# A planned kernel on one core: a transfer queue in the plan, filler products as plan steps, and a newly searched order

## Chip, core and metric

The kernel runs on one core of a Trainium2 chip. The metric is the device time of one execution in microseconds (us); the median over the runs of a comparison is quoted. A single-core program's run is called slow here when it is more than 1.5% above the fastest run of the same kernel in the same comparison, otherwise fast. Ratios between kernels are computed from the mean time of the fast runs of one kernel over the mean of the fast runs of the other, from the same rounds on the same chip. They are therefore not quite the ratio of the medians that are quoted beside them.

## The reference

A recurrent attention over 4 batches, 8 heads, 768 positions and 48 channels feeds a token mixer:

```
for t in range(S):
    cur   = outer(u * k[t], v[t])
    y[t]  = r[t] @ (state + cur)
    state = w[t] * state + outer(k[t], v[t])
x     = y, heads side by side                        # 4 x 768 x 384
W     = (x @ w_q) @ (x @ w_k)^T / sqrt(64)
out   = relu(W @ x) @ w_out
```

The inputs r, k, v and w are float32; the output is 4 x 768 x 384 float32.

## The kernel before

The positions are cut into twelve units of 256 (three for each batch; numbered 0 to 11 here). Per unit there are four loads of 384 KB (w, k, r, v into wg, kg, rg, vg, three buffers each). ScalarE takes the logarithm of w (step f_ln, tile lw), TensorE sums it over positions (f_cw), and from that come the decays en and ep, the scaled and transposed KT and RT, the products A of KT and RT, their masked form AM, the state SB, the output y and the mixer input X. After the third unit of a batch come the mixer's products T, mx and fp, and the stores.

The order of all instructions on all engines is fixed on the host by a list scheduler. A step has an engine, an estimated duration, a rank and the steps that it needs; buffers are rings.

```python
class Plan:
    def add(self, eng, dur, rank, fn, after=(), fill=None, read=(), lag=100, mode=0, behind=None):
        ...
    def order(self):
        ...                       # of the ready steps of a free engine, the lowest rank starts
```

Each engine executes its steps strictly in the planned order. The plan decides once which step comes before which.

```python
def load(b, i, tl, ap):
    nc.sync.dma_start(out=view(tl, 0, [[D2, H], [1, D2]]),
        in_=ap[b, :, ds(i * U, U)].rearrange("h (p j) d -> p h (j d)", j=2))
...
add("SP", 1250 + (900 if n == 0 else 0), "load", lambda: load(b, i, wg, w),
    fill="wg", got=g["wg"], lag=2000)
# ... kg, rg and vg likewise
def f_ln():
    nc.scalar.activation(view(lw, ...), view(wg, ...), ACT.Ln, bias=0.0, scale=math.exp(-MU))
add("A", 845, "ln", f_ln, fill="lw", got=g["lw"], use=[g["wg"]])
...
nc.vector.memset(Z, 0.0)
for _ in range(WARM):                             # nine fillers at the head, on the zero tile
    mm(PS[:, ds(0, 512)], Z[:, ds(0, C)], Z)
...
for s in plan.order():
    now["step"] = s
    s["fn"]()
```

Of the kernel before, what the change touches and what calls it, by code (L numbers as in the profile page):

```python
# [12 lines left out]
F32 = mybir.dt.float32  # L13
# [12 lines left out]
class Plan:  # L26
# [11 lines left out]
    def add(self, eng, dur, rank, fn, after=(), fill=None, read=(), lag=100, mode=0,  # L38
# [6 lines left out]
            self.reads(s, a)  # L45
        return s

    def reads(self, s, a, own=False):

        if not own:  # L50
            s["after"].append(a)
        if a["buf"] is not None:
            a["buf"]["left"] += 1
            s["reads"].append(a["buf"])

    def order(self):
# [22 lines left out]

        ready = [s for s in self.steps if not left[s["n"]]]  # L80
        running, done, eng_free, now = [], [], {}, 0
        mode = 0
        while ready or running:
            ready.sort(key=lambda s: (s["rank"] - self.stick * (s["eng"] == "PE"
                                                                and s["mode"] == mode), s["n"]))
# [1 line left out]
            while started:  # L87
                started = False
                for s in ready:
                    if s["behind"] is not None and "start" not in s["behind"]:  # L90
                        continue
                    if ready_at[s["n"]] > now or eng_free.get(s["eng"], 0) > now:
                        continue
                    if s["fill"] in ("w", "s"):
                        at = place(s["fill"])
                        if at is None:
                            continue
                        s["buf"]["bank"] = at
                        for x in range(at[0], at[0] + at[1]):
                            banks[x] = False  # L100
                    elif s["fill"] is not None:

                        ring, size = rings.setdefault(s["fill"], []), self.kinds[s["fill"]]
                        if len(ring) >= size and ring[-size]["left"]:
                            continue
                        ring.append(s["buf"])
                    took = s["dur"]
                    if s["eng"] == "PE":
                        took += self.switch * (s["mode"] != mode)
                        mode = s["mode"]  # L110
                    eng_free[s["eng"]] = now + took
                    heapq.heappush(running, (now + took + s["lag"], s["n"]))
                    s["start"] = now
                    done.append(s)
                    ready.remove(s)
                    started = True
                    break
# [6 lines left out]
            while running and running[0][0] <= now:  # L124
                t, n = heapq.heappop(running)
                s = self.steps[n]
                for buf in s["reads"]:
                    buf["left"] -= 1
                    if not buf["left"]:
                        for x in range(buf["bank"][0], sum(buf["bank"])) if "bank" in buf else ():  # L130
                            banks[x] = True
                for o in s["out"]:
                    left[o["n"]] -= 1
                    ready_at[o["n"]] = max(ready_at[o["n"]], t)
                    if not left[o["n"]]:
                        ready.append(o)
# [5 lines left out]
def kernel(  # L142
# [41 lines left out]
        return consts.tile(shape, dtype, name=name, tag=name)  # L184

    PS = ps.tile([C, 4096], F32, name="PS", tag="PS")
    WARM = 9
    NB = 3
    WG = [const([C, HW], F32, f"wg{i}") for i in range(NB)]
    RG = [const([C, HW], F32, f"rg{i}") for i in range(NB)]  # L190
# [35 lines left out]
    gv = const([C, 1], F32, "gv")  # L226

    nc.vector.memset(Z, 0.0)
    for _ in range(WARM):
        mm(PS[:, ds(0, 512)], Z[:, ds(0, C)], Z)  # L230
    nc.vector.memset(uT, 0.0)
    for hh in range(2):
        nc.scalar.dma_start(out=view(uT, hh, [[2, NP], [1, 1]], p0=hh * 64, pn=D),
# [37 lines left out]
    for j in range(2):  # L271
# [5 lines left out]

    NS = 2
    STEP = 100
    OFF = dict(load=-149, ln=901, c16=248, cw=-84, ex=-742, rT=1166, ks=886, qT=-1499, RT=731,  # L280
               KT=349, ptm=181, v16=-272, vp=114, vb=422, dps=395, vd=320, A=-667, am=556,
               kb=545, kd=-134, sn=-139, sb=91, y=278, x=-1392, xt=770, xts=808, qk=1219,
               qks=-111, T=-1307, mx=141, rl=-837, fp=-3204, os=-81, st=20, stick=99)
    ENG = dict(k16="PPPPPPPPPPDP", r16="PPPPPPPAPPDD", KT="DPPPPPPPPPPP", vb="AAAADAAAAAAA",
               kd="ADAAADADDADA", xts="DADAADAADAAA", qks="AAAAADAAAAAD", rl="DAAAAAAAADAD",
               os="AAAAAAAAAADD", dd="ADAADDDDAAAA", ks="DDADDDDDADAD")
    SPLIT = (0, B * NU - 1)
    NAMES = dict(A="ACT", D="DVE", P="POOL")

# [18 lines left out]
    def took(eng, cols, half=False, by=False):  # L308
        if eng == "A":
            return (265 if by else 180) + int(cols * 0.83)  # L310
        if eng == "P":
            return 100 + int(cols * 1.93)
        return (210 if by else 150) + int(cols * (0.52 if half else 1.04))

    def copy(eng, o, i, by=None):
# [13 lines left out]
        else:  # L329
            nc.vector.tensor_scalar_max(o, i, 0.0)  # L330

    def warm(at, count, after):

        def f():
            x = stile(F32, "warm")
            for _ in range(count):
                mm(x, ID16, Z)
        s_ = plan.add("PE", 215 * count, at, f, after, fill="s", lag=100)
        plan.reads(s_, s_, True)

    class Got:

# [10 lines left out]
    def unit(n, state, batch):  # L353
# [41 lines left out]
        def cols(cs, w_):  # L395
# [1 line left out]

        g = {x: Got() for x in ("wg kg rg vg lw k16 r16 v16 vp cw ep en kT rT ks qT RT KT ptm VB dps dd Vd"
                                " A0 A1 AM0 AM1 kb KD sn y xt XT qk").split()}
        add("SP", 1250 + (900 if n == 0 else 0), "load", lambda: load(b, i, wg, w), fill="wg", got=g["wg"], lag=2000)  # L400
        add("SP", 1250, "load", lambda: load(b, i, kg, k), fill="kg", got=g["kg"], lag=2000)
        add("SP", 1250, "load", lambda: load(b, i, rg, r), fill="rg", got=g["rg"], lag=2000)

        add("SP", 1250, "load", lambda: load(b, i, vg, v), fill="vg", got=g["vg"], lag=2000)

        def f_ln():
            nc.scalar.activation(view(lw, 0, [[64, H], [512, 2], [1, D]]),  # L407
# [4 lines left out]
        def f_c16(dst, src, e):  # L412
# [3 lines left out]
                   view(src, 0, [[D2, H], [D, 2], [1, D]]))  # L416
            return f
        e = ENG["k16"][n]
        add(e, 500 if e == "D" else 830, "c16", f_c16(k16, kg, e), fill="k16", got=g["k16"],
            use=[g["kg"]])  # L420
        e = ENG["r16"][n]
        add(e, 500 if e == "D" else 830, "c16", f_c16(r16, rg, e), more=1, fill="r16", got=g["r16"],
            use=[g["rg"]])

        def f_cw():
# [108 lines left out]
        for cs in fine:  # L534
            def f_vd(cs=cs):
                nc.gpsimd.tensor_tensor(  # L536
                    sb("Vd", [C, 2 * DM])[:, cols(cs, DM)], t["VB"][:, cols(cs, DM)],
                    view(t["dd"], cs[0] * H, [[1, len(cs) * H], [0, D]]), ALU.mult)
            add("P", took("P", DM * len(cs)), "vd", f_vd, more=2 * cs[0], fill="Vd", got=g["Vd"],
                cs=cs, use=[g["VB"], g["dd"]])  # L540

        for c in range(2):
# [178 lines left out]
        for ii in range(NU):  # L721
            m = b * NU + ii
            gm, gM, gf, go = Got(), Got(), Got(), Got()
            if end and ii == 0:
                warm(STEP * n + OFF["mx"] - 1, 2, Tall)

            def f_mx(ii=ii):
                t[f"mx{ii}"] = x = wtile("mx")
# [3 lines left out]
                       start=(dt != 1))  # L732
            add("PE", 330, "mx", f_mx, Ts + batch["wq"], more=6 * ii, fill="w", got=gm)

            if end and ii == NU - 1:
                warm(STEP * n + OFF["mx"] + 6 * ii + 1, 2, [gm.first])
            halves = each if end else both
            for p, cs in enumerate(halves):
                e = "AD"[p] if end else ENG["rl"][m]
# [23 lines left out]
            for p, cs in enumerate(halves):  # L763
# [15 lines left out]
                if end and ii == NU - 1 and p == 0:  # L779
                    add("A", 550, "st", f_st(nc.scalar), more=6 * ii, cs=cs, use=[go], lag=2000)  # L780
                else:
                    add("SP", 650 * len(cs), "st", f_st(nc.sync), more=6 * ii, cs=cs, use=[go],
                        lag=2000)

    state = {}
    batch = None
# [18 lines left out]
    for n in range(B * NU):  # L805
        if n % NU == 0:
            batch = {"X": {}, "qks": [], "wq": [], "xs": []}
        if n == 0:
            wl = plan.add("SP", 2500, 105, f_wld, lag=2000)
            state["ub"] = plan.add("POOL", 200, 12, f_ub)  # L810
            state["wts"] = plan.add("POOL", 1800, 120, f_wcast, [wl])
        unit(n, state, batch)
# [33 lines left out]
```

## Time and profile before

| | before |
|---|---|
| median of 3 runs (range) | 120.91 us (118.89 to 121.9) |
| profiled run; its span and mean TensorE clock | 119.73 us; 118.0 us, 0.952 |
| TensorE busy in the span | 101.0 us (86%) |
| TensorE idle from 20 to 108 us | 9.0 us |
| last load issued | 70.70 us |

The page and windows are shown and read in the prediction. The waits: who waited for whom; total us, times, longest.

```profile
ACT lw L407 <- DMA wg<-in_w_dram: 8.7, 6, 2.4
```

Then the queue of SyncE in time (start, us until its issue ended, what it moved): two stores, a third store, and the w loads of units 10 and 11.

```profile
44.37 1.60 SPq L774 DMA_DIRECT2D out_dram<-os  x2
...
49.93 0.38 SPq L774 DMA_DIRECT2D out_dram<-os  x1
...
61.17 1.20 SPq L213 DMA_DIRECT2D wg<-in_w_dram  x1
...
66.38 1.89 SPq L213 DMA_DIRECT2D wg<-in_w_dram  x1
```

And ScalarE's own timeline of lw for those two units, with some of its neighbours; the bracket is idle time of the engine just before, and what ended it.

```profile
63.27 1.02 ACT L438 ACTIVATE en<-PS 128x1024 bf16<-128x1024 f32 x1
64.19 1.04 ACT L444 ACTIVATE ep<-PS 128x1024 bf16<-128x1024 f32 x1
66.35 0.84 ACT L407 ACTIVATE lw<-wg 128x768 bf16<-128x768 f32 x1 [1.12 <-DMA wg<-in_w_dram]
67.10 0.78 ACT L318 CAST VB<-PS 128x768 bf16<-128x768 f32 x1
...
71.90 0.84 ACT L407 ACTIVATE lw<-wg 128x768 bf16<-128x768 f32 x1
```

So before also waits for loads on ScalarE, 8.7 us in six pieces, but near the end of the loads only 1.12 us, and the last not at all.

### The profile page before, as it was taken

To read this page: it belongs to the slowest core of one execution; us is meant where nothing else is said; L and a number is where in the kernel's file an instruction comes from. 1 tells how busy PE (TensorE), PEld (TensorE's weight loads), DVE (VectorE), ACT (ScalarE), POOL (GpSimd) and SP (SyncE) were. 2 spreads that over 40 slices of the span, in tenths; PEclk is the share of its full clock that TensorE was granted. 3 is DMA by queue.
4 is the path that set the end of the run, shared out by engine and by line. 5 is a ranking of instruction groups with operands and counts; after the bars stand their busy time and mean duration, and the time that the engine had idled before them with its cause. 6 is when DMAs were issued, how large, how long until landed. Compare 5 with 4: busy or idle time off the path is not lost. (4 is left out here: it accounts for less than half of the span.)

```text
span 118.0 us, 3685 instructions
## 1 busy us (share of the span) xinstructions
PE 101.0 (86%) x1496; PEld 69.8 (59%) x1496; DVE 89.9 (76%) x143; ACT 80.9 (69%) x120; POOL 75.5 (64%) x95
## 2 busy tenths in 40 slices
PE   5858988796987999793999389999999999998980
PEld 2344957473865666482878246667678776673440
DVE  6837897977798768979499696978789996761460
ACT  4375497786955698676899664758999638675630
POOL 6485789999996998883916999370794580050000
PEclk9985599999999999999999976999999999999998
DMA  2999999999999999999998999533120000523064
GB/s 55 306 316 314 320 292 250 313 288 280 315 293 285 310 244 237 363 341 249 244 280 225 319 273 272 138 133 133 43 96 0 6 0 0 190 85 133 0 230 172
DMA packets 54865, 24.61 MB, mean 209 GB/s; under 512 B 51392, under 2 KB 54848, under 8 KB 54848
## 3 DMA queue, kind: packets, MB, share of 16 engines
q1 hardware_dynamic: 54288, 24.19, 72.5%
q10 hardware_dynamic: 560, 0.20, 0.7%
q8 instruction: 11, 0.18, 0.6%
q14 instruction: 6, 0.05, 0.1%
HBM read 19.66 MB, written 4.72 MB: 207 GB/s over the span
## 5 line engine op out<-in xcount | busy, mean ns | idle before, releaser
L554 DVE TENSOR_TENSOR AM<-PS,US 128x1024 bf16<-128x1024 f32 x24 | 28.8, 1218 | 4.0 <-PE PS L173 3.1
L487 POOL TENSOR_TENSOR KT<-ks,en 128x1024 bf16<-128x1024 bf16 (+1 forms) x12 | 23.8, 1988 | 2.3 <-ACT en L438 1.1
L536 POOL TENSOR_TENSOR Vd<-VB,dd 128x768 bf16<-128x768 bf16 (+1 forms) x14 | 18.0, 1292 | 9.3 <-ACT dd L318 8.8
L407 ACT ACTIVATE lw<-wg 128x768 bf16<-128x768 f32 x12 | 10.2, 846 | 8.8 <-DMA wg<-in_w_dram 8.7
L438 ACT ACTIVATE en<-PS 128x1024 bf16<-128x1024 f32 (+1 forms) x14 | 12.6, 904 | 4.8 <-PE PS L173 3.4
L641 DVE SCALAR_TENSOR_TENSOR X<-PS,gx,Vd 128x768 bf16<-128x768 f32 (+1 forms) x13 | 12.4, 953 | 4.4 <-PE PS L173 2.2
L173 PEld LDWEIGHTS <-KT 48*128 48x128 bf16 (+1 forms) x272 | 11.0, 100 | 5.7 <-POOL KT L487 1.8
L501 POOL CAST v<-vg 128x768 bf16<-128x768 f32 x12 | 10.2, 854 | 5.9 <-PE PS L173 5.6
L415 POOL CAST k<-kg 128x768 bf16<-128x768 f32 x11 | 9.1, 824 | 7.4 <-PE PS L173 4.3
L173 PE MATMUL PS<-wo,MX 128*128 128x384 bf16 x72 | 13.3, 327 | 0.0
L600 DVE TENSOR_TENSOR SB<-PS,ptm 128x384 bf16<-128x384 f32 x20 | 11.0, 552 | 2.6 <-PE PS L173 1.8
L444 ACT ACTIVATE ep<-PS 128x1024 bf16<-128x1024 f32 (+1 forms) x14 | 12.9, 922 | 0.0
L318 ACT COPY os<-PS 128x768 f32<-128x768 f32 (+1 forms) x12 | 8.5, 722 | 4.4 <-PE PS L173 4.4
L328 ACT ACTIVATE MX<-PS 128x768 bf16<-128x768 f32 (+1 forms) x11 | 8.0, 724 | 4.5 <-PE PS L173 4.5
L173 PE MATMUL PS<-qk,ts 128*128 128x256 bf16 x36 | 10.2, 406 | 0.1
L173 PE MATMUL PS<-RT,KT 48*128 48x128 bf16 x192 | 8.8, 227 | 1.5 <-POOL KT L487 1.5
L173 PE MATMUL PS<-CM,lw 64*128 64x128 bf16 x192 | 7.6, 221 | 2.8 <-DVE X L641 1.8
L173 PE MATMUL PS<-VB,AM 128*128 128x48 bf16 x192 | 8.5, 185 | 1.6 <-DVE AM L554 1.0
L318 ACT CAST VB<-PS 128x768 bf16<-128x768 f32 x11 | 8.8, 802 | 1.4 <-POOL wq L797 0.7
L173 PEld LDWEIGHTS <-AM 128*128 128x128 bf16 x192 | 7.5, 97 | 3.2 <-issue 1.1
L173 PEld LDWEIGHTS <-MX 128*128 128x128 bf16 x72 | 6.5, 98 | 4.7 <-issue 0.3
L173 PEld LDWEIGHTS <-lw 64*128 64x128 bf16 x192 | 5.7, 96 | 5.5 <-issue 3.1
(81 smaller groups left out, 213.3 us busy)
## 6 DMA issues: line engine op xcount, KB each, us to landing
wg<-in_w_dram SPq DMA_DIRECT2D x12, 384.0 KB, 5.1
kg<-in_k_dram SPq DMA_DIRECT2D x12, 384.0 KB, 5.3
rg<-in_r_dram SPq DMA_DIRECT2D x12, 384.0 KB, 5.6
vg<-in_v_dram SPq DMA_DIRECT2D x12, 384.0 KB, 5.4
out_dram<-os SPq DMA_DIRECT2D x9, 384.0 KB, 3.7
out_dram<-os SPq DMA_DIRECT2D x5, 192.0 KB, 2.0
wof<-in_moe_w_out_dram SPq DMA_DIRECT2D x1, 576.0 KB, 4.5
out_dram<-os ACTq DMA_DIRECT2D x1, 192.0 KB, 2.2
```

The lines of the kernel that those rows point to most:

```text
L173: nc.tensor.matmul(o, l, rr, start=start, stop=stop, skip_group_check=True, is_transpose=trans)
L318: nc.scalar.copy(o, i)
L407: nc.scalar.activation(view(lw, 0, [[64, H], [512, 2], [1, D]]), view(wg, 0, [[D2, H], [D, 2], [1, D]]), ACT.Ln, bias=0.0, scale=math.exp( ...
L415: op(view(dst, 0, [[64, H], [512, 2], [1, D]]), view(src, 0, [[D2, H], [D, 2], [1, D]]))
L438: nc.scalar.activation(sb("en", [C, 1024])[:, cols(cs, 512)], t["cw"][:, cols(cs, 512)], ACT.Exp, bias=0.0, scale=-1.0)
L444: nc.scalar.activation(view(ep, cs[0] * NP * EW + 66, [[EW, NP * len(cs)], [-65, 2], [1, 64]]), t["cw"][:, cols(cs, 512)], ACT.Exp, bias=0 ...
L487: e.tensor_tensor(sb("KT", [C, 1024])[:, cols(cs, 512)], t["ks"][:, cols(cs, 512)], t["en"][:, cols(cs, 512)], ALU.mult)
L501: nc.gpsimd.tensor_copy(view(sb("v16", [C, 2 * DM]), 0, [[D, H], [DM, 2], [1, D]]), view(vg, 0, [[D2, H], [D, 2], [1, D]]))
L536: nc.gpsimd.tensor_tensor(sb("Vd", [C, 2 * DM])[:, cols(cs, DM)], t["VB"][:, cols(cs, DM)], view(t["dd"], cs[0] * H, [[1, len(cs) * H], [0 ...
L554: nc.vector.tensor_tensor(view(sb(f"AM{c}", [C, 1024]), 0, [[C, 8], [1, C]]), view(t[f"A{c}"], 0, [[C, 8], [1, C]]), view(US, 0, [[0, 8], ...
L600: nc.vector.tensor_tensor(view(x, 0, [[D, H], [1, D]]), view(t[f"sn{c}"], 0, [[D, H], [1, D]]), view(t["ptm"], c * 8, [[1, 8], [0, D]]), A ...
L641: nc.vector.scalar_tensor_tensor(view(X["t"], (2 * i + c0) * DM, [[DM, ncs], [1, DM]]), view(t["y"], c0 * 512, [[512, ncs], [1, DM]]), gx, ...
```

## The change

The intent is to give the plan a better picture of the transfers (issue, a queue of at most three, one transfer after another, landing), to keep TensorE busy with filler products where it would wait in the fill and the tail, and to search a new set of ranks and engine choices for this plan. Some estimated durations of VectorE and GpSimd steps change too. Cut to its core:

```diff
+    def dma(self, issue, dur, rank, fn, after=(), fill=None, read=()):
+        i = self.add("SP", issue, rank, fn, after, fill, read, lag=0)
+        m = self.add("DQ", dur, 0, self.nothing, [i], lag=0)
+        return i, self.add(f"L{m['n']}", 1950, 0, self.nothing, [m], lag=0)
...
+                    if s["eng"] == "SP" and queued >= 3:
+                        continue
...
-    WARM = 9
-    for _ in range(WARM):
-        mm(PS[:, ds(0, 512)], Z[:, ds(0, C)], Z)
...
-    OFF = dict(load=-149, ln=901, ...)           # all ranks and the engine choices ENG
+    OFF = dict(load=-152, ln=1232, ...)
...
-    def warm(at, count, after):
-        def f():
-            x = stile(F32, "warm")
-            for _ in range(count):
-                mm(x, ID16, Z)
+    def warm(count, dur, after=()):
+        def f():
+            mm(stile(F32, "warm"), ID16, Z)
+        for _ in range(count):
+            s_ = plan.add("PE", dur, 1 << 20, f, after, fill="s", lag=0)
...
-        add("SP", 1250 + (900 if n == 0 else 0), "load", lambda: load(b, i, wg, w), fill="wg", got=g["wg"], lag=2000)
+        for tile_, ap, name in ((wg, w, "wg"), (kg, k, "kg"), (rg, r, "rg"), (vg, v, "vg")):
+            issue, land = plan.dma(450, 1180 + 600 * (name == "wg" and n == 0), STEP * n + OFF["load"],
+                                   lambda tile_=tile_, ap=ap: load(b, i, tile_, ap), fill=name)
...
+            first = plan.add("PE", 900, -1 << 20, plan.nothing)
+            warm(26, 215, [warm(8, 430, [first])])
```

A filler now has the lowest priority (rank 1 << 20): the plan starts one whenever nothing else is ready on TensorE.

More of the change, by code (lines that the diff above doesn't have):

```diff
@@ L46, in add, with nothing @@
         return s
+    def dma(self, issue, dur, rank, fn, after=(), fill=None, read=()):
+        i = self.add("SP", issue, rank, fn, after, fill, read, lag=0)
+        m = self.add("DQ", dur, 0, self.nothing, [i], lag=0)
+        return i, self.add(f"L{m['n']}", 1950, 0, self.nothing, [m], lag=0)
+    def nothing(self):
+        pass
     def reads(self, s, a, own=False):
@@ L81, in order @@
         running, done, eng_free, now = [], [], {}, 0
-        mode = 0
+        mode = queued = 0
         while ready or running:
@@ L107, in order @@
                     took = s["dur"]
+                    if s["eng"] == "SP":
+                        queued += 1
+                        for o in s["out"]:
+                            o["rank"] = now
                     if s["eng"] == "PE":
@@ L126, in order @@
                 s = self.steps[n]
+                if s["eng"] == "DQ":
+                    queued -= 1
                 for buf in s["reads"]:
@@ L279 @@
     STEP = 100
-    OFF = dict(load=-149, ln=901, c16=248, cw=-84, ex=-742, rT=1166, ks=886, qT=-1499, RT=731,
-               KT=349, ptm=181, v16=-272, vp=114, vb=422, dps=395, vd=320, A=-667, am=556,
-               kb=545, kd=-134, sn=-139, sb=91, y=278, x=-1392, xt=770, xts=808, qk=1219,
-               qks=-111, T=-1307, mx=141, rl=-837, fp=-3204, os=-81, st=20, stick=99)
-    ENG = dict(k16="PPPPPPPPPPDP", r16="PPPPPPPAPPDD", KT="DPPPPPPPPPPP", vb="AAAADAAAAAAA",
-               kd="ADAAADADDADA", xts="DADAADAADAAA", qks="AAAAADAAAAAD", rl="DAAAAAAAADAD",
-               os="AAAAAAAAAADD", dd="ADAADDDDAAAA", ks="DDADDDDDADAD")
+    OFF = dict(load=-152, ln=1232, c16=380, cw=-22, ex=-532, rT=1051, ks=1101, qT=-1108, RT=587,
+               KT=-193, ptm=-254, v16=-363, vp=175, vb=283, dps=183, vd=300, A=-1242, am=620,
+               kb=202, kd=-731, sn=84, sb=105, y=316, x=-1752, xt=1179, xts=1244, qk=908,
+               qks=-118, T=-358, mx=392, rl=-1057, fp=-2818, os=96, st=605, stick=9)
+    ENG = dict(k16="PPPPPPPPAPPA", r16="PPPPAPDPAPPD", KT="DPPDPPPPPPPP", vb="AAAAAAAAAAAA",
+               kd="ADAAAADDDDDD", xts="DADDDDAAAAAA", qks="AAAAAAAAAAAA", rl="DAAADAAAAAAA",
+               os="AAAAAAAAAAAA", dd="ADAADAAAAAAA", ks="DDDDDDDDAAAD")
     SPLIT = (0, B * NU - 1)
@@ L311, in took @@
         if eng == "P":
-            return 100 + int(cols * 1.93)
+            return 140 + int(cols * 1.94)
         return (210 if by else 150) + int(cols * (0.52 if half else 1.04))
@@ L330, in relu @@
             nc.vector.tensor_scalar_max(o, i, 0.0)
-    def warm(at, count, after):
+    def warm(count, dur, after=()):
         def f():
-            x = stile(F32, "warm")
-            for _ in range(count):
-                mm(x, ID16, Z)
-        s_ = plan.add("PE", 215 * count, at, f, after, fill="s", lag=100)
-        plan.reads(s_, s_, True)
+            mm(stile(F32, "warm"), ID16, Z)
+        for _ in range(count):
+            s_ = plan.add("PE", dur, 1 << 20, f, after, fill="s", lag=0)
+            plan.reads(s_, s_, True)
+        return s_
     class Got:
@@ L399, in unit @@
                                 " A0 A1 AM0 AM1 kb KD sn y xt XT qk").split()}
-        add("SP", 1250 + (900 if n == 0 else 0), "load", lambda: load(b, i, wg, w), fill="wg", got=g["wg"], lag=2000)
-        add("SP", 1250, "load", lambda: load(b, i, kg, k), fill="kg", got=g["kg"], lag=2000)
-        add("SP", 1250, "load", lambda: load(b, i, rg, r), fill="rg", got=g["rg"], lag=2000)
-        add("SP", 1250, "load", lambda: load(b, i, vg, v), fill="vg", got=g["vg"], lag=2000)
+        for tile_, ap, name in ((wg, w, "wg"), (kg, k, "kg"), (rg, r, "rg"), (vg, v, "vg")):
+            issue, land = plan.dma(450, 1180 + 600 * (name == "wg" and n == 0), STEP * n + OFF["load"],
+                                   lambda tile_=tile_, ap=ap: load(b, i, tile_, ap), fill=name)
+            issue["behind"] = state.get(name)
+            state[name] = issue
+            g[name].first, g[name].by = issue, {0: land, 1: land}
         def f_ln():
@@ L418, in unit @@
         e = ENG["k16"][n]
-        add(e, 500 if e == "D" else 830, "c16", f_c16(k16, kg, e), fill="k16", got=g["k16"],
+        add(e, 680 if e == "D" else 830, "c16", f_c16(k16, kg, e), fill="k16", got=g["k16"],
             use=[g["kg"]])
         e = ENG["r16"][n]
-        add(e, 500 if e == "D" else 830, "c16", f_c16(r16, rg, e), more=1, fill="r16", got=g["r16"],
+        add(e, 680 if e == "D" else 830, "c16", f_c16(r16, rg, e), more=1, fill="r16", got=g["r16"],
             use=[g["rg"]])
@@ L538, in f_vd @@
                     view(t["dd"], cs[0] * H, [[1, len(cs) * H], [0, D]]), ALU.mult)
-            add("P", took("P", DM * len(cs)), "vd", f_vd, more=2 * cs[0], fill="Vd", got=g["Vd"],
+            add("P", 185 + 646 * len(cs), "vd", f_vd, more=2 * cs[0], fill="Vd", got=g["Vd"],
                 cs=cs, use=[g["VB"], g["dd"]])
@@ L724, in unit @@
             if end and ii == 0:
-                warm(STEP * n + OFF["mx"] - 1, 2, Tall)
+                warm(16, 215, Tall)
             def f_mx(ii=ii):
@@ L733, in unit @@
             add("PE", 330, "mx", f_mx, Ts + batch["wq"], more=6 * ii, fill="w", got=gm)
-            if end and ii == NU - 1:
-                warm(STEP * n + OFF["mx"] + 6 * ii + 1, 2, [gm.first])
             halves = each if end else both
@@ L781, in unit @@
                 else:
-                    add("SP", 650 * len(cs), "st", f_st(nc.sync), more=6 * ii, cs=cs, use=[go],
-                        lag=2000)
+                    issue, land = plan.dma(
+                        400, 570 * len(cs), STEP * n + OFF["st"] + 6 * ii, f_st(nc.sync),
+                        [go.by[c] for c in cs])
+                    plan.reads(land, go.first, True)
     state = {}
@@ L808 @@
         if n == 0:
-            wl = plan.add("SP", 2500, 105, f_wld, lag=2000)
+            wl = plan.dma(1500, 2500, 105, f_wld)[1]
+            first = plan.add("PE", 900, -1 << 20, plan.nothing)
+            warm(26, 215, [warm(8, 430, [first])])
             state["ub"] = plan.add("POOL", 200, 12, f_ub)
```

## The prediction

> **What bounds the kernel now.** I read the page first: shares, then the forty slices.
>
> ```profile
> span 118.0 us, 3685 instructions
> PE 101.0 (86%) x1496; PEld 69.8 (59%) x1496; DVE 89.9 (76%) x143; ACT 80.9 (69%) x120; POOL 75.5 (64%) x95
> PE   5858988796987999793999389999999999998980
> POOL 6485789999996998883916999370794580050000
> PEclk9985599999999999999999976999999999999998
> DMA  2999999999999999999998999533120000523064
> ```
>
> TensorE is the fullest engine, and the chain that ended last lies 44% on it, with about 5% more on the other engines together. But its 86% is not uniform: the row of tenths has holes in the first eight slices and again near the slice of the 3. The clock row falls twice, to 5 in the fill and to 7 and 6 in the middle. The transfers fill the first 22 slices, yet loads end before slice 30 and 40 us of work follow, so they don't set the end.
>
> Next I cut the span into windows. The first ones are spaced 3.41 us apart, because the fall and the rise of the clock lie on such a grid. Columns: stretch, length and busy TensorE time (matmuls), granted clock, DMA share, GB/s.
>
> ```profile
> 4.47:7.88 3.41, 1.63 (x26) 0.98 1.15 310
> 7.88:11.29 3.41, 2.80 (x27) 0.50 1.15 317
> 11.29:14.70 3.41, 3.41 (x54) 0.52 1.16 319
> 20.00:40.00 20.00, 16.62 (x287) 1.00 1.09 298
> 40.00:60.00 20.00, 17.28 (x303) 1.00 1.00 283
> 60.00:65.85 5.85, 5.85 (x116) 1.00 0.97 258
> 65.85:69.27 3.42, 1.19 (x28) 0.99 1.10 301
> 69.27:72.68 3.41, 3.41 (x34) 0.51 0.97 256
> ```
>
> A window with TensorE half idle (1.63 of 3.41) is followed by two at half clock. The stall at 66 us (1.19 of 3.42) is followed by one. From 20 to 108 us the idle time is 3.38 + 2.72 + 2.23 + 0.28 + 0.39 = 9.0 us. So after 20 us the kernel is bound by TensorE, with 9 us of holes and one cold window.
>
> The waits of TensorE in that stretch, and its own timeline around the largest, say what opens the holes:
>
> ```profile
> PE PS L173 <- ACT KD L320: 2.7, 2, 2.0
> PE PS L173 <- DVE X L641: 2.4, 2, 1.8
> PE PS L173 <- POOL KT L487: 1.5, 2, 1.1
> 67.90 0.62 PE L173 MATMUL PS<-CM,lw 64*128 64x128 bf16 x16 [1.83 <-DVE X L641]
> ```
>
> The 1.83 us hole is a matter of order: GpSimd waited 3.12 us for TensorE before 62.62, then ran two casts, v, Vd and KT in a row; X had to wait for Vd, and TensorE for X.
>
> [...] both falls fit one 3.41 us grid, and the first nine fillers start 0.42 us apart[...]. [...] KT of 128x512 took VectorE 1.00 us while GpSimd was casting at 8.47, and 0.41 at 9.99 while it was idle. [...]
>
> **The change, part by part.**
>
> 1. *Plan timings and the queue model.* These are host-side; they run nothing on the chip, only order it. The first 34 transfers stand in the same order; the first three batch stores move behind nine more loads. The store order at the end is the same. Worth 0 by itself.
>
> 2. *Fillers in the fill.* Nine at the head become 34, twelve of them before the first real product (cw), then groups of 2, 4, 2, 1, 4, 4, 1, 1, 1 and 2 among the first products. They now use the identity ID as the loaded operand; before, the head used only the zero tile. The zero tile is ready at about 1.2 us, but ID is written by GpSimd at 3.70 to 3.99 us of the trace. The plan allows 0.9 us for this. So the twelve start at about 4.05, not 1.24. On the grid of this run they are cold until 7.88: nine at 0.427, three at 0.215, ending near 8.5; cold throughout, near 9.2. cw stood at 5.39, so it comes 3.1 us later. Two fillers more and the k transposes start near 9.5, not 7.01 (+2.5).
>    From there the chain is warm: ks 0.69, KT 0.41 twice, qT 0.68, RT 0.41, putting the first A product at about 12.8 against 11.57, and its product AM about 1.0 us later than 12.22. After that before still runs cold to 14.70 and after does not. I followed both orders to the third unit's cw: before issues it at 18.42; after reaches it near 18.5, but with vp (0.43) and xt (0.33) of unit 1 still undone, and four more fillers behind it (4 x 0.215 = 0.86). Net cost of the fill: 0.1 + 0.8 + 0.8 = 1.7 us. The fillers repay only the cold windows, not their own late start.
>
> 3. *The new order and engines.* By row counts times the mean of each form, GpSimd gives up one KT (2.155), one k cast (0.824) and one r cast (0.823): -3.8 us, most of it in the first seven units, where its row reads 8 and 9. ScalarE takes two k casts and an r cast (3 x 0.83), a VB (0.80), a qk (0.48) and three dd (0.53), and gives two KD (2.21), an XT (0.81) and an MX (0.81): +0.5. VectorE takes two KD (1.50), an MX (0.96), an XT (0.55) and a KT (0.8 to 2), and gives a VB (0.95), a k (0.55), a qk (0.55) and three dd (0.51): +1.3 or more. None comes near TensorE's sum. Between dependent products I counted the TensorE work that the order leaves (warm durations of dense groups). Short of what cw to A, kT to A, A to y and y to xt need: before lacks 6.5 us in all, after 1.1; part of that is fillers, which is waiting in another name. Units 3 to 11 mostly have more room in after. I take half of the 9.0 us of holes as saved (4.5; choice, not measured), and the cold window at 69 us (half of 3.41 = 1.7).
>
> 4. *The tail.* Three fillers stand before the last nine mx products (two before), one before the last eighteen, twelve after them. The gap there was 108.12 to 108.84, room for three; the one adds 0.2 us. The last twelve take 12 x 0.215 = 2.6 us from about 114.0, ending before the store's landing at 118. Cost 0.2.
>
> Sum against the profiled run of 119.73: +1.7 - 4.5 - 1.7 + 0.2 = -4.3, so 115.4. A searched order never behaves on the chip quite as planned, and its start is misplaced by 3 us, so I keep less than half of the gain: **117.2 us**, 3% under the median of 120.91.
>
> **Rivals.**
> - *The fillers only cost.* Other engines' waits don't shrink, 22 fillers of 0.215 (4.7 us) after the head become delay, and half-clock windows merely move. For it: the 3 us late start, and that fillers sit ahead of ready products. Against: they are in the place of waits that the trace has, and cold windows are gone. Time about 121.
> - *The order is everything.* The holes nearly close, the fill is absorbed since transfers are the limit there anyway (three waits of lw for the load, 3.4 us between 12 and 45 us). Time about 114.
> - *Another engine bounds.* VectorE at 91 us of work with X and AM on the path, or GpSimd, opens new holes as fast as old ones close; [...] For it: VectorE is busy 7.6 to 8.8 of each 10 us between 20 and 70 us already and gets work. Time 118 to 120.
>
> **Range and chances.** The middle is 117.2, between the sum 115.4 and the third rival. Low 114.3 is the second rival, high 120.3 just short of the first. The limit for 2% under 120.91 is 118.5, some 1.3 above my middle: faster 0.62, same 0.30, slower 0.08.
>
> **What would show it.** Fillers starting near 4.0 and cw near 8.5: part 2 right; near 1.3: my reading of ID is wrong and the time is about 3 us better. No clock below 9 between 9 and 20 us, and none in the middle: the cold windows are saved. Idle TensorE time from 20 us to the last mx near 4.5, not 9.0: part 3 right; near 9: wrong, and the time is about 121. GpSimd's sum near 72 and VectorE's near 91. The twelve fillers at the end finishing before the last store lands. The prediction fails if the search worked on a false start and the whole order is late by it, or if a new stall of over 2 us appears.

## The result, and the profile after

On the same chip after took 123.38 us (median of 4 runs, 122.88 to 124.37) and before 119.9 (4 runs, 118.02 to 121.9). The ratio of the fast runs is 1.0426, with a 95% interval of 1.0284 to 1.0567. The change is **slower by about 4%** (2.9% in the medians, as two of the four runs of before count as slow). The prediction of 117.2 us and its range to 120.3 were wrong.

The page of after: header, the shares, then busy tenths in forty slices of 3.07 us (PEclk is the granted TensorE clock in tenths of full speed, so 5 is half clock), and the chain that ended last.

```profile
span 122.7 us, 3760 instructions
PE 106.6 (87%) x1533; PEld 72.9 (59%) x1533; DVE 93.0 (76%) x142; ACT 81.4 (66%) x124; POOL 72.4 (59%) x92
PE   0699997996979998999994459899899999988995
...
PEclk9999999999999999999999855999999999999999
DMA  2999999999999989979999994000031500423054
...
PE 51%; DVE 16%; POOL 10%; issue 9%; DMA 9%; ACT 3%; SPq 0%; POOLq 0%; DVEq 0%; ACTq 0%
```

The clock row shows no 5 before the middle. Its 9 in the second and third slice is no measured full clock, though: the first ten fillers take 4.17 us (4.03 to 8.20), 0.42 us each, about half the pace of the last twelve (2.75 us in all), and the trace's clock record begins only then. So the chain is warm from about 8.2 us on, before the first cw, as intended. But TensorE's row has a valley of 4, 4, 5 in slices 22 to 24 (from 64 to 74 us), the clock row falls to 5 there, and the chain that ended last now lies 9% on transfers. These are the two w loads of units 10 and 11:

```profile
61.28 5.62 DMA wg<-in_w_dram
...
66.95 4.86 DMA wg<-in_w_dram
```

Before's chain has no transfer in that stretch; it is followed back only to 56.1 us (its shares add up to 49%), so it says nothing about earlier loads. The windows around the valley lie on the 3.41 us grid on which this run's clock fell and rose (columns as in the prediction's windows, with all engines):

```profile
66.23:69.64 3.41, 1.08 (x33) 1.01 (x32) 0.73 (x3) 2.46 (x3) 1.18 (x2) 1.00 1.03 274
69.64:73.05 3.41, 1.27 (x12) 0.58 (x9) 1.87 (x3) 1.16 (x3) 2.90 (x5) 0.50 1.12 308
73.05:76.46 3.41, 3.41 (x34) 2.65 (x32) 2.14 (x3) 1.80 (x3) 2.41 (x3) 0.50 0.56 153
20.00:108.00 88.00, 77.87 (x1252) 56.72 (x1246) 74.05 (x97) 65.33 (x96) 59.37 (x61) 0.96 0.71 198
```

TensorE's idle time from 20 to 108 us is 88.00 - 77.87 = 10.1 us, where before had 9.0 and the prediction 4.5; and two windows run at half clock. That is not peculiar to the profiled run: all four runs of after have a mean clock of 0.972, which is about 6.8 us at half clock in each, or two windows (estimated from clock and span). TensorE's waits name what opened the valley:

```profile
PE PS L190 <- ACT VB L332: 2.9, 1, 2.9
...
PE PS L190 <- ACT dd L332: 1.5, 1, 1.5
PE PS L190 <- DVE X L656: 1.1, 3, 0.6
```

The two new ones are ScalarE's. Its timeline there:

```profile
59.23 1.04 ACT L459 ACTIVATE ep<-PS 128x1024 bf16<-128x1024 f32 x1
...
62.16 0.91 ACT L422 ACTIVATE lw<-wg 128x768 bf16<-128x768 f32 x1
62.90 0.23 ACT L332 COPY dd<-PS 128x16 f32<-128x16 f32 x1
66.98 0.84 ACT L422 ACTIVATE lw<-wg 128x768 bf16<-128x768 f32 x1 [3.85 <-DMA wg<-in_w_dram]
67.73 0.78 ACT L332 CAST VB<-PS 128x768 bf16<-128x768 f32 x1
68.41 1.03 ACT L453 ACTIVATE en<-PS 128x1024 bf16<-128x1024 f32 x1
71.89 0.84 ACT L422 ACTIVATE lw<-wg 128x768 bf16<-128x768 f32 x1 [2.46 <-DMA wg<-in_w_dram]
72.64 0.15 ACT L332 COPY dd<-PS 128x16 f32<-128x16 f32 x1
```

and TensorE's:

```profile
68.56 0.56 PE L190 MATMUL PS<-VB,AM 128*128 128x48 bf16 x16 [2.85 <-ACT VB L332]
...
72.85 0.59 PE L190 MATMUL PS<-ID,KT 128*128 128x128 bf16 x4 [1.52 <-ACT dd L332]
```

ScalarE stands idle for 3.85 us in front of lw of unit 10, because its load has not landed. Behind it stands VB. Its input, the product of v and PM, was complete at about 65.05 us (issued at 64.55, 0.50 long), and TensorE needs VB at once. The same happens 5 us later with lw of unit 11, dd and VB. SyncE's queue shows the loads:

```profile
57.90 2.96 SPq L787 DMA_DIRECT2D out_dram<-os  x3
61.28 0.71 SPq L229 DMA_DIRECT2D wg<-in_w_dram  x1
...
66.95 1.08 SPq L229 DMA_DIRECT2D wg<-in_w_dram  x1
```

The w loads of units 10 and 11 were issued at 61.28 and 66.95 us; before issued them at 61.17 and 66.38. **The data come hardly later than they did. What has changed is how early ScalarE stands waiting for them.** In both orders the VB of unit 7 and the en of unit 9 stand right behind lw of unit 10. But after is done with the en and ep of unit 8 about 5 us sooner (ep at 59.23 against 64.19), so it stands at this lw from 63.1 us and loses 3.85, where before comes to it at 65.2 and loses 1.12. And lw of unit 11 stands three places earlier: before runs ep of unit 9 and two small steps ahead of it, after puts it right behind en of unit 9 and loses another 2.46.

The plan's own start times explain the order; they are computed on the host and are no measurements. After's plan has lw of units 10 and 11 at 60.4 and 63.6 us, before's plan (1250 ns a load) at 61.9 and 66.9. On the chip after ran them at 66.98 and 71.89, so 6.6 and 8.3 us later than planned (before: 4.5 and 5.0). Lw of unit 9, which did not wait for its load, was already 2.8 us late (planned 59.4, run at 62.16). One term of the rest is the pace: the plan takes 1.18 us per 384 KB, while at the 279 GB/s that the trace shows from 20 to 62.82 us 393,216 bytes take 1.41 us. Which part of the change put the two lw there, the queue model or the new ranks, was not run. Planned anew on the host, with 1.41 us a load and all ranks kept, lw of unit 10 comes to stand behind VB of unit 7 and en and ep of unit 9, while lw of unit 11 still stands ahead of VB of unit 8; no kernel was run with that plan.

Head and tail of the profile read as was foreseen, and the lines that show it are these: the fillers' late start with the first cw, and the last fillers, which end at 121.4 of 122.7 us.

```profile
4.03 4.80 PE L190 MATMUL PS<-Z,ID 128*128 128x512 bf16 x12 [4.03 <-POOL ID L283]
8.77 0.62 PE L190 MATMUL PS<-CM,lw 64*128 64x128 bf16 x16
...
118.68 2.75 PE L190 MATMUL PS<-Z,ID 128*128 128x512 bf16 x12
```

Following single products through both traces locates the loss: after's first cw is 3.4 us behind before's; the first A products of units 1 to 6 are 0.2, 1.1, 3.4, 0.6, 0.3 and 1.3 behind; that of unit 7 is 5.7 behind, and the last fp 4.7. The delay of the fill is mostly made up by 60 us; the loss arises between there and 77 us.

### The profile page after: what moved, and what is told of

It reads as the page before. It is cut to its first block, busy times and chain, and to the rows that moved or that the text cites. A ratio compares the mean times of both kernels' runs of the same rounds, so it can differ in the third digit from the quotient of the medians.

```text
span 122.7 us, 3760 instructions
## 1 busy us (share of the span) xinstructions
PE 106.6 (87%) x1533; PEld 72.9 (59%) x1533; DVE 93.0 (76%) x142; ACT 81.4 (66%) x124; POOL 72.4 (59%) x92
## 2 busy tenths in 40 slices
DMA packets 54866, 24.63 MB, mean 201 GB/s; under 512 B 51392, under 2 KB 54848, under 8 KB 54848
## 4 chain that ended last, share of the span: by engine, by line
PE 51%; DVE 16%; POOL 10%; issue 9%; DMA 9%; ACT 3%; SPq 0%; POOLq 0%; DVEq 0%; ACTq 0%
PE PS L190 51%; DMA wg<-in_w_dram 9%; DVE AM L569 7%; POOL KT L502 3%; DVE ks L336 2%; DVE SB L615 2%; DVE X L656 1%; POOL Vd L551 1%; DVE KT L502 1%; DVE qT L484 1%; POOL wq L812 1%; POOL v L516 1%; ACT ep L459 1%; DVE XT L336 1%; POOL PM L281 1%
## 5 line engine op out<-in xcount | busy, mean ns | idle before, releaser
L502 POOL TENSOR_TENSOR KT<-ks,en 128x1024 bf16<-128x1024 bf16 (+1 forms) x11 | 21.4, 1949 | 1.6 <-DVE ks L336 1.3
L190 PE MATMUL PS<-Z,ID 128*128 128x512 bf16 x50 | 15.1, 428 | 4.2 <-POOL ID L283 4.0
L508 POOL TENSOR_TENSOR ptm<-ep,MB 128x16 f32<-128x16 bf16 (+1 forms) x14 | 3.8, 278 | 15.0 <-DVE SB L615 7.2
L190 PEld LDWEIGHTS <-ID 128*128 128x128 bf16 x66 | 6.5, 106 | 10.1 <-POOL ID L283 4.0
L332 ACT CAST VB<-PS 128x768 bf16<-128x768 f32 x12 | 9.7, 806 | 1.3 <-PE PS L190 1.1
L342 ACT ACTIVATE MX<-PS 128x768 bf16<-128x768 f32 (+1 forms) x10 | 7.1, 715 | 5.2 <-PE PS L190 5.1
L336 DVE COPY ks<-PS 128x1024 bf16<-128x1024 bf16 x9 | 6.2, 684 | 4.6 <-PE PS L190 4.5
```

Of the source, the lines that this page charges most:

```text
L190: nc.tensor.matmul(o, l, rr, start=start, stop=stop, skip_group_check=True, is_transpose=trans)
L332: nc.scalar.copy(o, i)
L336: nc.vector.tensor_copy(o, i)
L502: e.tensor_tensor(sb("KT", [C, 1024])[:, cols(cs, 512)], t["ks"][:, cols(cs, 512)], t["en"][:, cols(cs, 512)], ALU.mult)
```

## The experiments

Three accounts were set against each other. **T**: lw standing early on ScalarE in the fixed order, before its transfer has landed, holds back VB, dd and en, and through them TensorE. **O**: the order itself, as searched, is no better, whatever the transfers do. And the **fill**: the identity tile comes at 4 us, so all starts about 3 us late, or the fillers delay real work. Twelve kernels ran, in three groups, each group on one chip with its own runs of before.

| run | what | median us | before there | ratio of fast runs (95%) |
|---|---|---|---|---|
| a_zero | after, fillers load the zero tile | 125.27 | 119.39 | 1.0482 (1.0369 to 1.0595) |
| a_silent | after, no fillers in the fill | 124.77 | 119.39 | none given |
| a_lwlate | after, two lw later | 119.07 | 119.39 | 0.998 (0.9885 to 1.0074) |
| a_stlate | after, three stores later | 122.6 | 119.39 | 1.0296 (1.0154 to 1.0438) |
| a_noload | after, loads of three units only | 118.38 | 120.05 | 0.9974 (0.9848 to 1.0099) |
| b_noload | before, loads of three units only | 115.93 | 120.05 | 0.977 (0.9628 to 0.9911) |
| a_both | after, five lw and three stores later | 121.22 | 120.05 | 1.0227 (1.0071 to 1.0383) |
| b_both | before, seven lw and three stores later | 117.9 | 120.05 | 0.9925 (0.9744 to 1.0106) |
| a_noload_zero | a_noload and a_zero | 115.29 | 119.14 | 0.9807 (0.9744 to 0.9871) |
| a_lwlate_zero | a_lwlate and a_zero | 118.88 | 119.14 | 1.0105 (1.0047 to 1.0162) |
| b_lwlate | before, seven lw later | 119.57 | 119.14 | 1.0137 (1.0069 to 1.0205) |
| b_best | b_both and fillers in the fill's holes | 117.79 | 119.14 | 0.9974 (0.9893 to 1.0056) |

In the last group before itself fell into two clusters (117.3 to 118.24 and 118.99 to 121.49), and its fast runs are the quick cluster and 118.99; in the second group only two of its seven runs are fast (117.88 and 119.35). So the ratios there flatter before against the medians. Both are given.

### a_zero: the fillers without the identity

```diff
-            mm(stile(F32, "warm"), ID16, Z)
+            mm(stile(F32, "warm"), Z[:, ds(0, C)], Z)
```

> The changed kernel with every filler loading the zero tile instead of the identity: same instructions, same order, but the head can start at 1.2 us instead of 4.03. Theory S (the late start is the loss): cw moves from 8.8 to about 5.4 and the end follows by about 3 us, so 120.3 against 123.4. Theory T (the loss is made at 66 to 73 us, where ScalarE stands in its fixed order at lw and waits for the last two w transfers, which come when the transfers allow): the start moves but the end by less than 1 us, about 122.8.

It was correct, at 125.27 us, and so no faster than after. Its profiled run was a slow one (127.13). In it the first cw came at 6.1 instead of 8.77 us, but the first A product of unit 3 is already 1.3 us behind that of after. ScalarE waited 14.4 us for w loads instead of 8.7, TensorE lost 1.85 us to a k cast that waited for its load, with half clock behind it (0.79 on average from 36 to 44 us), and its later waits for VB (2.3 us) and dd (1.6) stayed. The earlier start was taken back by the transfers. The late start is thus not what makes after slow.

### a_silent: no fillers in the fill

```diff
-            warm(26, 215, [warm(8, 430, [first])])
+            warm(26, 215, [warm(8, 430, [first], False)], False)   # False: emits nothing
```

> The changed kernel whose 34 fillers of the fill emit nothing; everything else in the same order. Theory S and the rival that fillers only cost: cw at 5.4, up to 34 x 0.215 = 7 us of TensorE work gone, but half-clock windows return between 8 and 15 us; end 2.5 to 4 us earlier, about 120. Theory T: the stall at the last w transfers stays, end within 1 us of 123.4.

It was at 124.77 us (122.27 to 125.09, three of the four runs slow, the profiled one among them). cw came 3.4 us sooner than in after; by unit 3 the lead was 0.3 us. ScalarE waited 12.1 us for w loads. TensorE itself waited 5.3 us for one lw, and its clock fell to half from 27.8 to 34.6 us. The one fast run, 122.27, is level with after's lowest, 122.88. So the products added in the fill don't make after slow either, as far as one fast run can say.

### a_lwlate: lw of units 10 and 11 stand later on ScalarE

```diff
+        steps = plan.order()
+        lns = [s for s in steps if s["fn"].__name__ == "f_ln"]
+        cws = [s for s in steps if s["fn"].__name__ == "f_cw"]
+        for ln, cw in list(zip(lns, cws))[10:]:
+            steps.remove(ln)
+            at = next(x for x, s in enumerate(steps) if s["start"] >= cw["start"] - 2500)
+            steps.insert(at, ln)
-        for s in plan.order():
+        for s in steps:
```

The two instructions stand 4 and 9 places later in ScalarE's order (the text below says 3 and 9); no other instruction changes its place.

> The changed kernel with only two ScalarE instructions moved: lw of units 10 and 11 stand 3 and 9 places later, behind VB, dd and en which TensorE waits for. Theory T: the waits of 3.85 and 2.46 us on ScalarE go, TensorE's waits for VB (2.9) and dd (1.5) go, and with them the half-clock windows at 70 to 76: 3 to 4.5 us less, about 119.5. Theory S: no change, 123.4.

It was at **119.07 us**, 4.3 us under after in the medians and level with before (0.998). No fall of the clock is in its fast runs (mean 1.0, against 0.972 in every run of after); only fillers at the start go at half pace (twelve in 4.24 us, where the last twelve of after take 2.75). ScalarE's timeline at the same place:

```profile
64.68 0.80 ACT L332 CAST VB<-PS 128x768 bf16<-128x768 f32 x1 [1.96 <-PE PS L190]
...
68.01 0.80 ACT L332 CAST VB<-PS 128x768 bf16<-128x768 f32 x1 [1.31 <-PE PS L190]
68.70 0.85 ACT L422 ACTIVATE lw<-wg 128x768 bf16<-128x768 f32 x1
```

VB now runs at 64.68 instead of 67.73 us and waits for TensorE and not for a transfer. Two instructions out of 3760 hold the whole loss against before. This is what T says.

### a_stlate: the first three stores behind the last loads

```diff
+        early = [s for s in steps if s["eng"] == "SP" and s["fn"].__name__ == "f"][:3]
+        last = [s for s in steps if s["eng"] == "SP" and s["fn"].__name__ == "<lambda>"][-1]
+        # early are taken out and put back behind last
```

> The changed kernel with the first three output stores moved behind the last loads in the transfer queue: the loads of units 10 and 11 are issued some 3 us earlier. Theory T: the two lw waits shrink from 6.3 to about 3 us, end about 2 us earlier, 121.4. Theory S: no change, 123.4.

Its four runs scattered over 119.03, 121.76, 123.44 and 125.88 us, with a single fast one. That one is level with before's 119.39, so the ratio, 1.0296, can't be that of the fast run, and nothing is rested on it. In the fast run, which was profiled, both lw ran at 63.66 and 67.51 us without a wait, although they stood where the change puts them. The other runs were not profiled; why they lost 3 to 7 us is open. Their mean clocks, 0.986, 0.972 and 0.959 against 1.0, amount to about one, two and three windows at half clock (estimated from clock and span), and what opened them was not shown. That the waits depend on when the loads land, and that this differs from run to run, would fit, but was not shown either. Moving the stores can remove the wait, but not dependably.

### a_noload and b_noload: without the transfers

```diff
 def load(b, i, tl, ap):
+    if b * NU + i >= 3:
+        return
```

These give wrong results: every unit after the third computes on old data. The work on the engines is the same.

> The changed kernel without the 36 loads of units 3 to 11 (they compute on the data of units 0 to 2: a wrong result on purpose), order on the engines unchanged. Theory T (the new order is good, but was searched with transfers that land too early): without transfers it runs near its plan, 113 to 115 us, and below the kernel before without loads. Theory O (the order itself is worse): it stays above the kernel before without loads.

> The kernel before without the same 36 loads (wrong result on purpose). Theory T: it gains less than the changed kernel does, since its order waits less on transfers: 115 to 118. Theory O: it is the faster of the two, below 114.

a_noload took 118.38 us. lw of the last unit stands where the change puts it, and does not wait:

```profile
66.39 0.84 ACT L424 ACTIVATE lw<-wg 128x768 bf16<-128x768 f32 x1
```

Against after that is 5.0 us in the medians. a_lwlate, with all loads, runs within 0.5 us of it at every unit. The two moves thus recover nearly all that transfers cost the new order. But b_noload took 115.93 us: without transfers the new order was still 2.45 us slower than the old one, where T alone had expected it to be ahead. T explains the loss against before; something else had eaten the gain that the order was searched for.

### a_noload_zero: is that rest the late start?

> The changed order with no loads after the third unit (wrong result on purpose, as a_noload) and the fillers loading the zero tile, so that they and cw start early. Without transfers the new order was still 2.45 us behind the old one. If the late start of the first product (3.2 us later) is that rest, nothing else can absorb the earlier start here: 115.4 to 116.2, level with b_noload's 115.93. If the rest lies in the order itself, the time stays near a_noload's 118.4, and the early start is again taken back by other waits.

It took 115.29 us, 3.1 under a_noload. In its trace the first cw comes 2.7 us sooner than in a_noload, and from unit 5 on nearly all products come 2.9 us sooner, to the last fp. With nothing to absorb it, the late start costs about 3 us to the end. What is left of the new order against the old one, both starting early and both without transfers, is 115.29 against 115.93: **0.6 us, and these two ran in different groups**, so hardly more than nothing. By their ratios to before, 0.9807 and 0.977, even the sign turns. O is right to this extent: the order had little to give.

### a_lwlate_zero: both mended, with the transfers

> The changed kernel with both faults mended: lw of the last two units moved behind the work that TensorE needs, and fillers on the zero tile. Theory that the transfers absorb any earlier start: 119.0, as a_lwlate, with the waits of lw and of the casts for loads grown by 2 to 3 us before unit 5. Rival, that start and order add up: 116.5 to 117.5. In either case under the changed kernel's 123.4 by more than 4 us.

It was at 118.88 us, against 119.07 of a_lwlate. The early start is worth 3 us without transfers and 0.2 with them. The lead of 2.1 us holds to about 30 us; at 36 us it turns into a lag of 0.8. There GpSimd and TensorE show:

```profile
35.31 0.82 POOL L430 CAST k<-kg 128x768 bf16<-128x768 f32 x1 [2.23 <-DMA kg<-in_k_dram]
...
36.20 0.90 PE L190 MATMUL PS<-ID,k 128*128 128x128 bf16 x8 [1.98 <-POOL k L430]
```

In a_noload_zero the same product starts without a wait:

```profile
33.69 0.61 PE L190 MATMUL PS<-ID,k 128*128 128x128 bf16 x8
```

The start came earlier; this load did not come in time for it. The wait of 1.98 us is followed by a stretch at half clock (0.96 on average from 20 to 60 us, or about 3.2 us at half clock, estimated from that average), which is how the lead becomes a lag.

### a_both and b_both: one rule for both orders

In each kernel, any lw (from unit 1) planned more than 2.0 us ahead of its cw moves to 2.0 us ahead, and the first three stores go behind the last load. In after seven lw meet the rule, and five of them change place (units 1, 7, 8, 10 and 11); in before seven move (units 5 to 11). The texts below say four and three, which is wrong; the order on the host and the traces show it: b_both has lw of unit 6 at 46.99 and of unit 10 at 79.53 us, before at 39.30 and 66.35.

```diff
+        for ln, cw in list(zip(lns, cws))[1:]:
+            if ln["start"] < cw["start"] - 2000:
+                steps.remove(ln)
+                at = next(x for x, s in enumerate(steps) if s["start"] >= cw["start"] - 2000)
+                steps.insert(at, ln)
+        # and the three stores as in a_stlate
```

> The changed kernel with both repairs: lw never more than 2 us of the plan ahead of its cw (four of twelve move on ScalarE), and the first three stores behind the last loads. Theory T: at or under a_lwlate's 119.1, about 117.5, as the repairs act on the same stall and so do not add. Theory S: 123.4.

> The kernel before with the same two rules (three lw and three stores move). Theory T: its lw waits for transfers (8.7 us on ScalarE, of which TensorE sees less than 2) matter little, its stores cost the last loads about 3 us: 1 to 2 us less than 119.4, about 118. If the rules only repair the new order, 119.4.

a_both took 121.22 us, worse than a_lwlate with two moves. Its first cw was at 9.1 us (8.2 in a_lwlate), as its twelve fillers took 5.13 us, all at half pace, where a_lwlate's took 4.24; this slower start accounts for about 0.9. At the last fp product the lag on a_lwlate is 1.9 us; it grows in small steps at units 2, 6 and 9. The causes of those, the three further lw among them, were not taken apart. b_both took 117.9 us, with its waits of lw for loads down from 8.7 to 4.4 us. Its fast runs are not clearly faster than before's, but its median is 1.8% under it.

### b_lwlate and b_best: is there a version that beats both?

b_lwlate is b_both without the moved stores:

```diff
-        early = ...
-        steps[at:at] = early
```

> The kernel before with only three of lw moved later on ScalarE, the stores where they were; b_both (stores too) had 117.9. If the three early stores cost nothing in the old order, 117.9; if they are what was worth something, 119.5 to 120. Its waits of lw for loads should be near 4.4 us as in b_both.

It moves the same seven lw, not three. It took 119.57 us, no better than before (119.14). Its lw waits fell to 3.4 us, and the time did not. In its profiled run, which was slow, TensorE waited 2.65 us for X at 67 us, longer than the 1.83 of before: the hole that the prediction had shown, a GpSimd queue of casts and Vd, was still there. In before's own trace that chain is v, Vd and KT on GpSimd, while the VB behind lw of unit 10 comes later, at 67.10. So in the old order the waits of lw were hardly on the path; what b_both has over before would then lie in the stores, or in both together, which is not shown.

b_best adds fillers to b_both, in the place of waits that its trace shows in the fill:

```diff
-    WARM = 9
+    WARM = 11
+        pe = [s for s in steps if s["eng"] == "PE"]
+        pad = {id(pe[x]): count for x, count in ((1, 4), (2, 1), (3, 2))}
         for s in steps:
             now["step"] = s
+            for _ in range(pad.get(id(s), 0)):
+                mm(PS[:, ds(s["buf"]["bank"][0] * 512, 512)], Z[:, ds(0, C)], Z)
             s["fn"]()
```

Each filler writes the bank that the step behind it is about to overwrite, so it needs neither a buffer nor a wait of its own.

> b_both with fillers where the fill's holes are: 11 instead of 9 at the head, then 4, 1 and 2 ahead of the first k transposes, r transposes and KT transposes, all on the zero tile and in the place of waits that the trace has (0.5, 1.0, 0.3 and 0.8 us). If the cold windows of the fill cost time, the slow runs among the five should vanish and the median fall by 0.5 to 1.2 us to 116.7 to 117.4; if the loads absorb the fill, 117.9 with the wait moved to lw.

It was at 117.79 us, the best correct kernel: 1.1% under before in the medians (119.14), and well under after's 123.38. By the fast runs against before's quick cluster it is 0.9974, so whether it beats before is unclear. The fillers themselves gave nothing that these runs resolve (117.9 to 117.79, in different groups).

## Why the prediction was wrong

**Part 1 failed first.** It set the queue model to "worth 0 by itself", since it runs nothing on the chip, and the reading of the profile had said of the transfers that "they don't set the end". The plan, with its timing of loads, is what places lw in ScalarE's fixed order. After's plan has lw of units 10 and 11 6.6 and 8.3 us before they could run, and VB and dd stand behind them while ScalarE waits 3.85 and 2.46 us. Two instructions moved back gave 4.3 us in the medians, so the term that was put at 0 measured about +4.3 (how much of it the queue model and how much the ranks brought stays open). The reading of the chain had a gap as well: its shares add up to 49%, so half of the span was not on it. The transfers don't set the end by being last; they set the earliest time of units 4 to 11, and an order that runs ahead of them waits.

The trace of after shows what the fixed order costs: VB stood 2.85 us of TensorE's time behind an lw without data. The prediction did not reckon with that. It counted ScalarE's load only as a sum (+0.5 us), never as an order.

**Part 3, the sum, failed by that.** It took half of 9.0 us of holes as saved (-4.5) and the cold window at 69 us too (-1.7). Measured: holes of 10.1 us, and in place of one cold window two, from 69.64 to 76.46. Of the -4.5, some was real but not to be had: with the two lw moved, TensorE's idle time from 20 to 108 us is 6.9 us and the clock full, so about 2.1 of 4.5 and the whole of the cold window came true. That a_lwlate is still only level with before is because two limits stand close together: starting late, it loses some 3 us to the start; starting early (a_lwlate_zero), it loses as much to the loads. Only without either was it 115.29. That it is so close to the sum of 115.4 is luck, as that kernel has no loads and an early start, which the sum did not assume. The prediction's own count of slack, 6.5 against 1.1 us, looked at TensorE's dependent products and not at what loads feed. The step from 115.4 to 117.2 is misdescribed too: against 119.73 it keeps 2.5 of 4.3 us, more than half of the gain.

**Part 2 was right in its mechanism.** The fillers started at 4.03 us (said: 4.05), cw at 8.77 (8.5), and no clock under 9 fell between 9 and 60 us. The first A product came at 13.45 (said: about 12.8) and the third unit's cw at 19.25 (near 18.5). The net of +1.7 at the end of the fill can't be checked as a number of its own. The late start costs 3 us where nothing else binds, and 0.2 where transfers do (a_noload_zero and a_lwlate_zero); in after against before it shows as +0.2 to +3.4 until 60 us. The rival that the fill is absorbed "since transfers are the limit there anyway" was right about that, and wrong about the rest.

**Part 4 and the sums were right.** The last twelve fillers ended at 121.4 of 122.7 us; GpSimd's sum was 72.4 (said: 72), VectorE's 93.0 (said: near 91).

**The rivals.** "The fillers only cost" came nearest in time, at 121, but for a reason that a_silent speaks against. "Another engine bounds" had said that new holes open as fast as old ones close. One did open, on ScalarE instead of VectorE or GpSimd, and through a transfer: TensorE waited 2.85 us for VB, and two windows at half clock followed. The last sentence of the prediction names both ways to fail, the false start and the new stall. The chances did not: 0.08 for slower was far too little for a newly searched order, whose plan I could have compared with the trace of before, where lw already waited 8.7 us for loads.

**What stays open:** why a_stlate's runs scatter by 7 us; what a_both loses beyond 0.9 us; whether the three stores alone give b_both its gain; whether the queue model or the new ranks put the two lw where they stand; and whether b_best is truly faster than before.

## What to carry to other kernels

On an engine that executes in order, as ScalarE did here, a step that waits for a transfer belongs behind what other engines need sooner: standing ahead of it cost 4.3 us here. To move every such step later is no rule, though: with more of them moved a_both was slower than a_lwlate (121.22 against 119.07, other lw and stores moved too), and b_lwlate gained nothing. Before trusting a searched order, compare its planned landing times with the chip's (here 1.18 against 1.41 us per 384 KB), because the error adds up over forty loads and the search spends every bit of slack that the model promises. An experiment without the transfers shows how much of a gain they leave.

## What the traces show of the clock and the loads

- Waits of TensorE of 1.83 us in before (1.19 of 3.42 us busy) and 1.98 us in a_lwlate_zero were followed by half clock. A wait of 1.98 us in before (54.14 to 56.12 us) and one of 2.33 in a_zero (to 31.08 us) were not, so the length of one wait doesn't draw the line. Nor does busy time alone: on the grids of their runs, a window with 1.73 us busy kept the full clock in a_zero (26.16 to 29.57 us), and one with 2.05 us lost it in b_both (25.74 to 29.15). At half clock windows of 1.27 us (after) and 2.80 us (before) were followed by another, and windows of 3.41 us (both) by full clock.
- When the head of ScalarE's queue waited for a transfer, that cost here 3.85 and 2.46 us of ScalarE, two windows at half clock, and 4.3 us of the kernel's time (after against a_lwlate).
- The loads here go in runs of 384 bytes (51,392 of 54,866 packets are under 512), at 279 GB/s from 20 to 62.82 us in after. The landing times for the plan have to be taken from a trace like this.
- How a load's landing time varies between runs of one kernel no single trace shows; the scatter of a_stlate (119.03 to 125.88 us) may have to do with it.
